# A gated feed-forward layer on one core: token halves in turn, weights read twice, x transposed on TensorE

## The chip, the core and the metric

The kernel runs on one core of a Trainium2 chip. The metric is the device time of one execution, in microseconds (us). Six runs of the kernel before have a median of 315.34 us (314.54 to 315.62). The execution that the profiler recorded took 315.47 us; from its first to its last recorded instruction (the span) it is 313.7 us.

## The reference

```
def _gelu(x):
    return jax.nn.gelu(x, approximate=True)

B, S, D, F = 32, 32, 1024, 3584        # x: (B, S, D); w_gate, w_up: (D, F); w_down: (F, D); all bf16

def reference(x, w_gate, w_up, w_down):
    return (_gelu(x @ w_gate) * (x @ w_up)) @ w_down
```

There are 1024 tokens (T). The gelu is the tanh form, which the kernel computes as G times a sigmoid of a cubic in G.

## The kernel before

Everything is laid out by hand for five engines. Each engine has its own program (`prog_sp`, `prog_pe`, `prog_act`, `prog_dve`), run in the order in which it is written; semaphores posted by `post` and awaited by `wait` tie them together. There is no planner: the order of the lines is the order of the work. All DMAs are issued from SP (SyncE), so they stand in one queue.

**Layout.** TensorE contracts over the partitions, so x is wanted transposed: `xT` holds 8 chunks of 128 features (DC = 8) by 1024 tokens. The hidden width 3584 is cut into 28 chunks of 128 (FC = 28). The weights of gate and up come in 7 groups of 4 chunks (GF = 4, NG = 7); a group is 1 MB of gate and 1 MB of up, read in pieces of 1 KB (4 x 128 columns of 2 bytes), and `wgu` holds two groups (NB = 2). `wd` holds all of w_down (7 MB, in 7 pieces), `hT` all of the hidden values.

**SP (L136 to L156).** The first instruction is one DMA that transposes all of x on the way in (L137). After it come, group by group, gate (L146), up (L147) and a piece of w_down (L134). From the third group on, SP first waits until TensorE has used the buffer (L141). At the end SP waits, for each block of 128 tokens, until both halves of its output have been copied to `osb` and writes 256 KB (L155).

**TensorE (L158 to L204).** It waits for x, then for each chunk f: it waits for the group's up weights (L165, which stand behind gate in the queue) and, from the third chunk on, until VectorE has finished chunk f-2 (L167). Then, for each of two halves of 512 tokens (`th`), 8 matmuls accumulate gate into one PSUM bank (L171) and 8 accumulate up into another (L176); each matmul loads 128x128 weights and streams 512 columns. Two chunks of two halves with two banks each fill the 8 banks. In the second stage, for each of 8 blocks of 128 tokens (`tc`) and each of 28 chunks, two matmuls (`dh` = 0, 1) of 512 columns add to two banks (L200). All in all there are 3 x 448 matmuls of 512 columns.

**ScalarE and VectorE (L206 to L265).** For one chunk and half: ScalarE squares G (L215), VectorE makes the cubic (L243), ScalarE takes the sigmoid (L223), VectorE multiplies by G (L253) and by U (L257) into `hT`. A chunk's two halves go through these steps side by side. At the end ScalarE copies the `dh` = 0 halves of the output out of PSUM (L230), VectorE the `dh` = 1 halves (L264).

## Time and profile before

| | us |
|---|---|
| median of six runs | 315.34 |
| the profiled execution, whole | 315.47 |
| its span, first to last instruction | 313.7 |
| TensorE busy with matmuls | 293.1 (93%) |
| VectorE busy | 115.7 (37%) |
| ScalarE busy | 73.0 (23%) |
| TensorE idle before its first matmul | 17.4 |
| moved by DMA | 26.42 MB |

In the profile PE is TensorE's matmuls and PEld its weight loads (which run beside matmuls), DVE is VectorE, ACT is ScalarE, POOL is GpSimd, SP is SyncE and SPq its queue of DMA issues. Matmuls are pipelined, so the mean duration of one (some 380 ns) is longer than the step from one to the next. The column of TensorE's granted clock stands at 1.00 through the whole span in this profile; at which of its levels the engine worked is therefore read from the steps between matmuls.

### The profile page before, as it was taken

The page shows a single profiled execution, that of the slowest core. Times are in us where ns is not written, and L with a number is a line of the kernel's source. Part 1 is how long each engine was busy: PE and PEld are TensorE (multiplying, and loading weights), DVE is VectorE, ACT ScalarE, POOL GpSimd, SP SyncE. Part 2 cuts the span into 40 slices and gives each one's busy share as a digit, 9 for nine tenths or more (in the row PEclk, how much of TensorE's full clock was granted, in tenths as well). Part 3 has the DMA queues.
Part 4 walks back from the last instruction along what each step waited for, and adds up shares of the span by engine and source line. Part 5 has one row for each costly group of instructions (what it writes and reads, how often), then busy time and mean ns, then how long its engine had stood idle before and what let it go on. Part 6 is the DMA issues. An engine that isn't in the chain of part 4 may idle for free.

```text
span 313.7 us, 3338 instructions
## 1 busy us (share of the span) xinstructions
PE 293.1 (93%) x1344; PEld 132.1 (42%) x1344; DVE 115.7 (37%) x176; ACT 73.0 (23%) x122; POOL 0.2 (0%) x4
## 2 busy tenths in 40 slices
PE   0079999999999999999999999999999999999995
PEld 0024444444444444444444444444444444444442
DVE  0004556666555566655556666554000000000000
ACT  1004233333223332322243333222000000000000
POOL 0000000000000000000000000000000000000000
PEclk9999999999999999999999999999999999999999
DMA  8995007401900750190065000000000000000000
GB/s 199 319 362 191 2 0 241 162 2 52 350 2 0 222 179 2 34 364 7 0 210 192 2 1 0 2 1 0 0 36 33 0 36 33 0 33 36 0 33 33
DMA packets 27647, 26.42 MB, mean 84 GB/s; under 512 B 8688, under 2 KB 23024, under 8 KB 27632
## 3 DMA queue, kind: packets, MB, share of 16 engines
q1 hardware_dynamic: 27632, 26.22, 26.0%
q8 instruction: 10, 0.16, 0.2%
q14 instruction: 5, 0.04, 0.0%
HBM read 22.02 MB, written 2.10 MB: 77 GB/s over the span
## 4 chain that ended last, share of the span: by engine, by line
PE 93%; DMA 3%; SPq 3%; DVE 0%; issue 0%
PE ps L171 31%; PE ps L176 31%; PE ps L200 31%; DMA wgu<-in_w_up_dram 3%; SPq L137 2%; DVE osb L264 0%; SPq L146 0%
## 5 line engine op out<-in xcount | busy, mean ns | idle before, releaser
L171 PE MATMUL ps<-xT,wgu 128*128 128x512 bf16 x448 | 107.5, 383 | 17.4 <-DMA wgu<-in_w_up_dram 17.4
L176 PE MATMUL ps<-xT,wgu 128*128 128x512 bf16 x448 | 107.1, 382 | 0.0
L200 PE MATMUL ps<-wd,hT 128*128 128x512 bf16 x448 | 96.9, 379 | 0.0
L243 DVE SCALAR_TENSOR_TENSOR tt<-sq,ps 128x512 f32<-128x512 f32 x56 | 38.5, 688 | 99.0 <-ACT sq L215 99.0
L171 PEld LDWEIGHTS ps<-xT,wgu 128*128 128x128 bf16 x448 | 44.1, 99 | 70.9 <-issue 19.0
L176 PEld LDWEIGHTS ps<-xT,wgu 128*128 128x128 bf16 x448 | 44.2, 99 | 54.1 <-issue 2.2
L200 PEld LDWEIGHTS ps<-wd,hT 128*128 128x128 bf16 x448 | 43.8, 98 | 52.9
L215 ACT ACTIVATE sq<-ps 128x512 f32<-128x512 f32 x56 | 33.4, 597 | 138.8 <-PE ps L171 138.8
L257 DVE TENSOR_TENSOR hT<-pp,ps 128x512 bf16<-128x512 f32 x56 | 38.5, 688 | 5.8
L253 DVE TENSOR_TENSOR pp<-sg,ps 128x512 f32<-128x512 f32 x56 | 38.1, 681 | 1.3 <-ACT sg L223 1.3
L264 DVE CAST osb<-ps 128x512 bf16<-128x512 f32 x8 | 5.5, 692 | 89.5 <-PE ps L200 89.5
L223 ACT ACTIVATE sg<-tt 128x512 f32<-128x512 f32 x56 | 35.0, 626 | 6.4 <-DVE tt L243 6.4
L230 ACT ACTIVATE osb<-ps 128x512 bf16<-128x512 f32 x8 | 4.8, 598 | 92.0 <-PE ps L200 92.0
L215 ACT ACT_TABLE_LOAD x1 | 1.3, 1283 | 0.7 <-PEq L305 0.7
L223 ACT ACT_TABLE_LOAD x1 | 1.3, 1283 | 0.0
L305 POOL MEMSET const-bfloat16-1.0<- 128x1 bf16 x1 | 0.1, 102 | 0.0
L305 POOL MEMSET const-uint8-127<- 128x1 uint8 x1 | 0.1, 102 | 0.0
L305 POOL MEMSET const-float32-1.0<- 128x1 f32 x1 | 0.1, 99 | 0.0
L305 POOL MEMSET const-float32-0.0<- 128x1 f32 x1 | 0.1, 98 | 0.2 <-issue 0.2
## 6 DMA issues: line engine op xcount, KB each, us to landing
wgu<-in_w_gate_dram SPq DMA_DIRECT2D x7, 1024.0 KB, 5.3
wgu<-in_w_up_dram SPq DMA_DIRECT2D x7, 1024.0 KB, 7.9
wd<-in_w_down_dram SPq DMA_DIRECT2D x7, 1024.0 KB, 9.9
out_dram<-osb SPq DMA_DIRECT2D x8, 256.0 KB, 2.0
xT<-in_x_dram SPq DMA_TRANSPOSE x1, 9.7
```

Source lines behind the costliest of these rows:

```text
L137: E.ins(lambda: sp.dma_start(xT[:, :, :], xf[:, :], transpose=True)).post(("x",), 16, c_x)
L171: E.ins(lambda: pe.matmul(G_bank(p, th), wslice(b, 0, dc)[:, fl:fl + 128], xT[:, dc, th * NT:(th + 1) * NT], start=(dc == 0), stop=(dc == ...
L176: E.ins(lambda: pe.matmul(U_bank(p, th), wslice(b, 1, dc)[:, fl:fl + 128], xT[:, dc, th * NT:(th + 1) * NT], start=(dc == 0), stop=(dc == ...
L200: E.ins(lambda: pe.matmul(ps[:, bank, 0:ND], hT[:, fc, tc * 128:(tc + 1) * 128], wd[:, fc, dh * ND:(dh + 1) * ND], start=(fc == 0), stop=( ...
L215: E.ins(lambda: act.activation(sq[:, r, :], G_bank(p, th), ACT.Square))
L223: E.ins(lambda: act.activation(sg[:, r, :], tt[:, r, :], ACT.Sigmoid, scale=K1))
L230: E.ins(lambda: act.activation(osb[:, tc, dh * ND:(dh + 1) * ND], ps[:, bank, 0:ND], ACT.Copy))
L243: E.ins(lambda: dve.scalar_tensor_tensor(out=tt[:, r, :], in0=sq[:, r, :], scalar=K2, in1=G_bank(p, th), op0=ALU.add, op1=ALU.mult))
L253: E.ins(lambda: dve.tensor_tensor(out=pp[:, r, :], in0=sg[:, r, :], in1=G_bank(p, th), op=ALU.mult))
L257: E.ins(lambda: dve.tensor_tensor(out=hT[:, f, sl], in0=pp[:, r, :], in1=U_bank(p, th), op=ALU.mult))
L264: E.ins(lambda: dve.tensor_copy(osb[:, tc, dh * ND:(dh + 1) * ND], ps[:, bank, 0:ND]))
L305: nc = _bacc.Bacc("TRN2", target_bir_lowering=False, num_devices=1)
```

## The change

The two halves of the tokens are no longer taken side by side within a chunk. The work of gate and up is cut into 56 units (`k`): all 28 chunks for the first 512 tokens, then all 28 for the second. A unit is 8 gate and 8 up matmuls of 512 columns, and uses two of four PSUM banks in turn. Since every weight is now needed in both passes, gate and up are read twice: 28 groups (`NQ`) of 2 chunks, each 512 KB of gate and 512 KB of up, in pieces of 512 B, in three buffers.

The first 512 tokens of x are loaded untransposed in four blocks of 128 tokens (into `osb`, which is free until the end), transposed on TensorE (32 transposes of 128x128 into four PSUM banks) and copied to `xT` by VectorE (2 copies) and ScalarE (2 copies). The second 512 tokens come by four DMA transposes, issued behind groups 6, 7, 9 and 10. Group 0 of the gate comes in two pieces, each with a semaphore. Before the transposes TensorE runs 7 (`NWARM`) matmuls on zeros; GpSimd and VectorE make the identity; ScalarE runs one small sigmoid.

The pieces of w_down are issued between the groups, each behind a wait for a unit. In the last block of tokens the two halves of the output are finished one after the other, and the second half as two matmuls of 256 columns per chunk in two banks, copied out by two engines; its two halves are written by two DMAs.

```diff
-    GF = 4 if FC % 4 == 0 else (2 if FC % 2 == 0 else 1)
-    NB = 2
+    NU = TH * FC
+    TBH = NT // 128
+    GF = 2 if FC % 2 == 0 else 1
+    NQ = TH * NG
+    NB = 3
+    WDP = 4
...
+        def kf(k):
+            return k % FC, k // FC
+        def G_bank(k):
+            return ps[:, 2 * (k % 2), 0:NT]
+        def U_bank(k):
+            return ps[:, 2 * (k % 2) + 1, 0:NT]
+        def psT(j):
+            return ps[:, 4 + j, :].bitcast(BF16)
...
+        XTQ = (6, 7, 9, 10)
...
+        def x_copy(E, kind, eng, th, j):
+            ndc = min(2, DC - 2 * j)
+            src = psT(j)[:, 0:ndc * 512].rearrange("p (a b) -> p a b", a=ndc)[:, :, 0:NT]
+            dst = xT[:, 2 * j:2 * j + ndc, th * NT:(th + 1) * NT]
+            E.wait(("T", th))
...
         def prog_sp(E, sp):
-            E.ins(lambda: sp.dma_start(xT[:, :, :], xf[:, :], transpose=True)).post(("x",), 16, c_x)
+            for pi, (t0_, n_, q_) in enumerate(XP):
...
+                    x_dma(E, sp, pi)
+            wg0_dma(E, sp)
+            wu0_dma(E, sp)
+            def group(q):
+                b = q % NB
+                if q >= NB:
+                    E.wait(("PEgrp", q - NB))
+                elif q >= 2:
+                    E.wait(("U",) + kf(q - 2))
...
+            def wd_part(j):
+                E.wait(("U",) + kf(min(NU - 1, 4 + 6 * j)))
...
+            for q in range(1, NQ):
+                if j < NWD and 4 + 6 * j < 2 * q - 5:
+                    wd_part(j)
+                    j += 1
+                group(q)
+                if q in XTQ:
+                    i = XTQ.index(q)
+                    t0 = NT + i * 128
+                    E.ins(lambda: sp.dma_start(xT[:, :, t0:t0 + 128], xf[t0:t0 + 128, :], transpose=True))
+                    E.post(("XC", 1, i), 16, c_x[TBH + i])
...
+            tc = TT - 1
+            E.wait(("E", tc, 0))
+            E.ins(lambda: sp.dma_start(of[tc * 128:(tc + 1) * 128, 0:ND], osb[:, tc, 0:ND])).post(("out", tc), 16, c_out)
+            E.wait(("E", tc, 1))
+            E.wait(("E2", tc, 1))
+            E.ins(lambda: sp.dma_start(of[tc * 128:(tc + 1) * 128, ND:D], osb[:, tc, ND:D])).post(("out2", tc), 16, c_out)
...
         def prog_pe(E, pe):
+            def transposes(th):
...
+                for tbl in range(TBH):
+                    E.wait(("x", tb))
+                    for dc in range(DC):
+                        E.ins(lambda: pe.transpose(psT(j)[:, col:col + 128],
+                                                   xnat[:, tb, dc * 128:(dc + 1) * 128], ident[:, :]))
+                E.post(("T", th))
+            def unit(k):
+                f, th = kf(k)
+                q = th * NG + f // GF
...
+                if k >= 2:
+                    E.wait(("D3",) + kf(k - 2))
...
+                    if f == 0 and th == 0 and dc % 2 == 0:
+                        E.wait(("XC", th, dc // 2))
...
+            E.wait(("zt",))
+            for i in range(NWARM):
+                E.ins(lambda: pe.matmul(ps[:, 7, :], zt[:, 0:128], zt[:, :], start=True, stop=True))
+            E.wait(("ident",))
...
+            transposes(0)
+            for k in range(NU):
+                unit(k)
...
+                order = [(fc, dh) for fc in range(FC) for dh in range(DH)]
+                if tc == TT - 1:
+                    order = [(fc, dh) for dh in range(DH) for fc in range(FC)]
...
+                    if tc == TT - 1 and dh == 1:
...
+                        E.ins(lambda: pe.matmul(ps[:, 5, 0:256], hT[:, fc, tc * 128:(tc + 1) * 128],
+                                                wd[:, fc, ND:ND + 256],
+                                                start=(fc == 0), stop=(fc == FC - 1)))
+                        E.ins(lambda: pe.matmul(ps[:, bank, 0:256], hT[:, fc, tc * 128:(tc + 1) * 128],
+                                                wd[:, fc, ND + 256:D],
+                                                start=(fc == 0), stop=(fc == FC - 1)))
...
         def prog_act(E, act):
+            E.wait(("zt",))
+            E.ins(lambda: act.activation(junk[:, 0:8], zt[:, 0:8], ACT.Sigmoid, scale=K1))
...
         def prog_dve(E, dve):
+            E.ins(lambda: dve.memset(zt[:, :], 0.0))
+            E.post(("zt",))
+            E.wait(("iota",))
+            E.ins(lambda: dve.tensor_scalar(ident[:, :], io[:, :], 128.0, None, op0=ALU.is_equal))
+            E.post(("ident",))
...
+            for k in range(NU):
+                dve_unit_a(E, dve, k)
+                dve_unit_b(E, dve, k)
```

## Rows read from the trace of the kernel before

**Rows 1.** The page: busy us, then busy tenths in 40 slices, then DMA packets.
```profile
PE 293.1 (93%) x1344; PEld 132.1 (42%) x1344; DVE 115.7 (37%) x176; ACT 73.0 (23%) x122; POOL 0.2 (0%) x4
...
PE   0079999999999999999999999999999999999995
...
DMA packets 27647, 26.42 MB, mean 84 GB/s; under 512 B 8688, under 2 KB 23024, under 8 KB 27632
```

**Rows 2.** The chain that ended last: start us, duration us, what, count.
```profile
0.73 7.55 SPq L137
...
8.97 8.25 DMA wgu<-in_w_up_dram
...
17.36 3.57 PE ps L171 x8
...
23.87 1.73 PE ps L171 x8
...
213.80 96.71 PE ps L200 x448
```

**Rows 3.** The start in order of time: start, duration, engine, line, operation, [idle before].
```profile
19.45 0.15 PEld L171 LDWEIGHTS ps<-xT,wgu 128*128 128x128 bf16 x1 [0.28 <-issue]
19.88 0.15 PEld L171 LDWEIGHTS ps<-xT,wgu 128*128 128x128 bf16 x1 [0.28 <-issue]
```

**Rows 4.** Stretches: us; PE, PEld, DVE, ACT, POOL busy; clock, DMA share, GB/s.
```profile
3.00:8.00 5.00, 0.00 (x0) 0.00 (x0) 0.00 (x0) 0.00 (x0) 0.00 (x0) 1.00 1.28 286
13.00:16.00 3.00, 0.00 (x0) 0.00 (x0) 0.00 (x0) 0.00 (x0) 0.00 (x0) 1.00 1.10 354
17.30:23.30 6.00, 5.94 (x15) 2.14 (x16) 0.69 (x1) 0.60 (x1) 0.00 (x0) 1.00 1.09 359
56.00:58.00 2.00, 2.00 (x11) 0.88 (x9) 1.90 (x3) 0.60 (x1) 0.00 (x0) 1.00 1.05 386
```

**Rows 5.** DMA issues of the page: names, count, KB each, median us to landing.
```profile
wgu<-in_w_gate_dram SPq DMA_DIRECT2D x7, 1024.0 KB, 5.3
wgu<-in_w_up_dram SPq DMA_DIRECT2D x7, 1024.0 KB, 7.9
out_dram<-osb SPq DMA_DIRECT2D x8, 256.0 KB, 2.0
```

**Rows 6.** One line's instructions: duration ns least/median/most, first and last start.
```profile
L155 SPq DMA_DIRECT2D out_dram<-osb x8: 332/332/360, 226.7 to 311.3; - x8
```

**Rows 7.** Groups by line: busy us, mean ns of one, idle before.
```profile
L171 PE MATMUL ps<-xT,wgu 128*128 128x512 bf16 x448 | 107.5, 383 | 17.4 <-DMA wgu<-in_w_up_dram 17.4
L200 PEld LDWEIGHTS ps<-wd,hT 128*128 128x128 bf16 x448 | 43.8, 98 | 52.9
L215 ACT ACTIVATE sq<-ps 128x512 f32<-128x512 f32 x56 | 33.4, 597 | 138.8 <-PE ps L171 138.8
L243 DVE SCALAR_TENSOR_TENSOR tt<-sq,ps 128x512 f32<-128x512 f32 x56 | 38.5, 688 | 99.0 <-ACT sq L215 99.0
L223 ACT ACTIVATE sg<-tt 128x512 f32<-128x512 f32 x56 | 35.0, 626 | 6.4 <-DVE tt L243 6.4
L253 DVE TENSOR_TENSOR pp<-sg,ps 128x512 f32<-128x512 f32 x56 | 38.1, 681 | 1.3 <-ACT sg L223 1.3
L257 DVE TENSOR_TENSOR hT<-pp,ps 128x512 bf16<-128x512 f32 x56 | 38.5, 688 | 5.8
```

**Rows 8.** The last chunk's second half, in order of time.
```profile
210.18 1.89 PE L171 MATMUL ps<-xT,wgu 128*128 128x512 bf16 x8
...
212.11 0.60 ACT L215 ACTIVATE sq<-ps 128x512 f32<-128x512 f32 x1 [2.86 <-PE ps L171]
```

**Rows 9.** The end in order of time.
```profile
308.82 1.67 PE L200 MATMUL ps<-wd,hT 128*128 128x512 bf16 x7
...
310.53 0.69 DVE L264 CAST osb<-ps 128x512 bf16<-128x512 f32 x1 [11.39 <-PE ps L200]
311.30 0.33 SPq L155 DMA_DIRECT2D out_dram<-osb  x1
```

## The prediction

> **What bounds the kernel now.** I read the page's busy times and slices first. TensorE is busy for 93% of the span, and its slices are full from the fourth to the last but one; the other engines are far from full [rows 1]. So there are two questions only: does TensorE ever run slower than it can, and what lies ahead of its first matmul and behind its last? The chain of waits answers both [rows 2]. SP spends 7.55 us issuing the one DMA that transposes x, then gate and up of group 0 have to land, and TensorE starts at 17.36. From 23.87 on, 8 matmuls take 1.73 us, and the 448 of the second stage take 96.71 us, which is 0.2159 us each. 1344 at this step are 290.13 us. From the first matmul to the end of the last (213.80 + 96.71 = 310.51) it is 293.15, so only 3.0 us are lost inside. The early rows say where: weight loads 0.43 us apart [rows 3] and 15 matmuls in 5.94 us [rows 4]. [...] (The column of the granted clock shows 1.00 there too, so I go by the steps.) The engine had worked for 5.9 us after standing still when it came up.

> The time is then a sum: 20.38 us ahead (17.36 + 3.02), 290.13 of matmuls, 3.19 behind the last matmul (313.7 - 310.51), and 1.77 outside the span (315.47 - 313.7). That makes 315.47, which is 0.13 above the median of 315.34.

> **The change part by part.**

> *The start.* The transposing DMA goes; in its place stand four loads of 256 KB, an issue of about 0.33 us each [rows 6]. A load of 1 MB lands 5.3 us after its issue [rows 5]; SP's first issue is at 0.73 [rows 2], so I put the fourth block at 6.0. Bounds: 2.0 us for the first 256 KB [rows 5] and three more at 386 GB/s [rows 4] give 4.8; half a microsecond of slower start gives 6.5.

> TensorE's own queue ahead of that: the zeros need one VectorE memset of 512 columns, which no row shows; between nothing and the 0.69 of VectorE's other 512-column work [rows 7], I take 0.5 and start the 7 warming matmuls at 1.3. At 0.427 each they end at 4.3. GpSimd's iota and the identity are hidden if both are done by then; iota is not in the trace, and with 0.69 for the identity it may take 2.9 us before it costs anything. By 4.3 two blocks of x lie ready. A transpose streams 128 columns: 0.107 us at the slow step, 0.054 at the fast one (a quarter of 0.427 and 0.216). All at the long step and without gaps, 32 of them end at 4.3 + 3.4 = 7.7; fast, the last eight end 0.4 behind the landing, at 6.4. I take 7.3, nearer the slow end, because the clock in before came up only 5.9 us after the first matmul, and 1.3 + 5.9 = 7.2.

> Copies of 1024 columns out of PSUM: between 0.60 and 1.38 us (a 512-column ScalarE operation, and twice a VectorE one [rows 7]); I take 1.2, and 0.1 for two hand-offs. Unit 0 starts at 8.6. Its fifth matmul needs the second pair of copies, 1.2 us later, while four fast matmuls last 0.86: a stall of 0.4 (0 if the clock is slow). Gate of group 0 has landed by about 7.5 and up by 9.0 to 9.7 (2 MB land 0.4 + 7.9 us after the first issue [rows 5], up to 0.7 more in smaller pieces), before 10.7, when it is first needed. For the clock I add 0.3. Ahead: 8.6 + 0.4 + 0.3 = 9.3 instead of 20.38.

> *The middle.* The number of 512-column matmuls stays 1344; gate and up are read twice. Group 1 and the later ones, w_down and the second half of x make 29.4 + 7.3 + 1.0 = 37.7 MB in 56 units of 3.454 us (16 steps), 193.4 us: 195 GB/s. Pieces of 512 B are not in the trace. The pieces on either side are: 1 KB (gate, up) at 354 GB/s, and x at 286 [rows 4], whose 8192 small packets (those below 512 B, of 8688 [rows 1]) carry 2.1 MB, 256 B each. So between 286 and 354, I take 300, and it is hidden. TensorE itself doesn't slow while DMA moves 386 GB/s: 11 matmuls begin or run in 2 us, all of it busy [rows 4]. [...] The four transposing DMAs take SP some 0.9 us each (an eighth of 7.55); behind each waits the next group, which is not due for another 6.9 us. SP has the same slack with the moved pieces of w_down: each waits for a unit that is already past when the wait is reached.

> *The new wait per unit.* Unit k waits for VectorE to finish unit k-2 (before it was a chunk of two halves, twice that distance). The chain after G's last matmul is 0.597 + 0.688 + 0.626 + 0.681 + 0.688 = 3.28 [rows 7] and four hand-offs of 0.04 (the matmuls end at 212.07, the square starts at 212.11 [rows 8]): 3.44. G ends 1.89 us into its unit, so the chain ends at 5.33 and unit k+2 begins at 6.91: 1.6 us to spare, cost nothing. Behind that wait stands all of TensorE's work; every microsecond of the chain beyond 1.6 would be paid up to 54 times.

> *The end.* The last block's second half runs as 56 matmuls of 256 columns. [...] After the last matmul: the copy of 512 columns (0.69 [rows 9]) becomes 256, between 0.35 and 0.69, I take 0.45; a write of 256 KB lands in 2.0 [rows 5], 128 KB saves up to 0.37, I take 1.7. Behind: 3.19 - 0.24 - 0.3 = 2.65.

> **Sum:** 9.3 + 290.13 + 0.07 + 2.65 + 1.77 = 303.9 us.

> **The rivals.**

> B, *the clock is still down when unit 0 begins.* Nothing in the trace says whether transposes, and the wait for copies after them, do what 5.9 us of dense matmuls did; the warming matmuls alone are 3.0 us. Then the transposes end at 7.7, unit 0 begins at 9.0, and 14 matmuls at the long step are paid again (2.95; the 0.4 of stall goes): 12.0 ahead, 306.6 us. For it: those 5.9 us. Against: TensorE would be without a long gap from 1.3 to 7.7. Its own range is 305.2 to 307.8.

> C, *transposes don't overlap.* A matmul lasts 383 ns while the step is 216 [rows 7]; if each transpose pays the 167 between them and 107 of columns, 32 cost 8.8 us, end at 13.1, and unit 0 begins at 14.4; with 0.4 of stall and half of the 3.0 for the clock, 310.9 us. A late identity looks the same. Against it: the loads and matmuls of all 1344 are pipelined. [...]

> D, *the weights come too late.* If the second reading and the 512 B pieces held DMA below 195 GB/s, every group after the first few would be waited for. At 184 GB/s (37.7 MB in 193.4 + 11.5 us) the gain is gone; at 150 the stage takes 251 us and the whole 362 us. Against it: 286 GB/s with pieces half as long.

> E, *the wait per unit bites a little*: 0.1 us over in each of 54 units is 5.4, 309.3 us; it needs a chain of 5.1 us where rows give 3.4.

> **How the numbers follow.** Forecast 0.48, B 0.32, C 0.11, E 0.05, D 0.03, and 0.01 for no change by several of these at once. Predicted: 303.9. The forecast's own range: early landing and fast copies (unit 0 at 7.3, no clock loss) give 302.2; the late ends of both (unit 0 at 9.4, 0.5 more for the clock) 305.2. The whole range reaches over B and its bounds, and leaves out most of C, E and D: 302.0 to 308.5. A measurement of this kernel can't tell less than about 0.2% (0.6 us) from no change. Forecast, B, C and E are faster: 0.96; within 0.2%: 0.01; D, slower: 0.03.

> **What would show it.** [...] Wrong: matmuls 0.43 us apart in units 0 and 1 (B); transposes more than 0.15 us apart (C); TensorE released by a weights DMA again and again, with the DMA slices full (D); short idle times before each unit that VectorE ends (E).

## The result, and the profile after

The changed kernel takes 303.35 us (median of 8 executions, 303.00 to 303.78), the one before 315.16 (16 executions): a ratio of 0.9628, with an interval of 0.9618 to 0.9638. 303.9 had been forecast. The profiled execution took 303.29 us, its span is 301.5. Of all the executions timed for this document one, with the old end described below, took 1802.93 us, and its run's ratio leaves it out.

The page of the changed kernel: busy us, then the slices, then DMA. They answer to [rows 1].

```profile
PE 296.6 (98%) x1411; PEld 137.8 (46%) x1411; DVE 122.5 (41%) x180; ACT 77.2 (26%) x125; POOL 0.4 (0%) x5
...
PE   8899999999999999999999999999999999999996
...
DMA packets 68065, 41.13 MB, mean 136 GB/s; under 512 B 5456, under 2 KB 63056, under 8 KB 68048
```

TensorE is full from the third slice on, with 14.7 MB more moved beside it. The chain of the changed kernel (start, duration, what) answers to [rows 2]:

```profile
2.11 0.43 SPq L183
...
3.61 6.67 DMA wgu<-in_w_up_dram
...
10.32 1.90 PE ps L293 x8
12.22 1.73 PE ps L287 x8
...
202.16 90.65 PE ps L343 x420
292.81 0.11 PE ps L336
```

From 12.22 on, 8 matmuls take 1.73 us, to the end of the first stage. Only the first up matmuls of unit 0 wait for a DMA. The chain goes from SP's issues through the landing of up to these matmuls; x, its transposes and its copies are not on it. The start of the changed kernel, in order of time, shows the pieces of its lead:

```profile
0.82 0.24 POOL L248 IOTA io<- 128x128 f32 x1 [0.38 <-POOLq L481]
0.86 0.27 DVE L414 MEMSET zt<- 128x256 uint32 x1 [0.86 <-PEq L481]
1.19 3.17 PE L301 MATMUL ps<-zt 128*128 128x512 bf16 x7 [1.19 <-DVE zt L414]
4.46 2.97 PE L263 MATMUL ps<-ident,osb 128*128 128x128 bf16 x32
7.47 1.29 DVE L194 COPY xT<-ps 128x1024 bf16<-128x1024 bf16 x2 [6.14 <-PE ps L263]
7.47 1.94 ACT L192 ACTIVATE xT<-ps 128x1024 bf16<-128x1024 bf16 x2 [5.23 <-PE ps L263]
8.22 1.90 PE L287 MATMUL ps<-xT,wgu 128*128 128x512 bf16 x8 [0.79 <-DVE xT L194]
10.32 1.90 PE L293 MATMUL ps<-xT,wgu 128*128 128x512 bf16 x8 [0.21 <-DMA wgu<-in_w_up_dram]
```

Unit 0 begins at 8.22 instead of 17.36, and at the short step: 8 matmuls take 1.90 us, of which the last lasts 0.38, so they begin 0.217 apart. Its 8 gate matmuls have run their steps at 9.95 (8.22 + 8 x 0.2159); its up matmuls begin at 10.32, a wait of 0.37 us (the 0.21 of the row counts from the last matmul's end). 8 steps before 10.32 is 8.59, the lead that answers to 20.38 before. Two stretches of the transposes show where the steps became shorter (us; PE and PEld busy with counts):

```profile
4.46:6.60 2.14, 2.14 (x21) 2.14 (x22) 0.00 (x0) 0.00 (x0) 0.00 (x0) 1.00 1.02 325
6.60:7.40 0.80, 0.80 (x14) 0.66 (x11) 0.00 (x0) 0.00 (x0) 0.00 (x0) 1.00 1.12 329
```

Some 20 transposes take 0.107 us each, a quarter of the 0.427 of the long step (in the kernel before, weight loads at 17.74 and at 22.86 lie 12 steps apart); the others come closer together. TensorE had worked since 1.19, with a pause of 0.1. The column of the granted clock stands at 1.00 in both stretches. That the long step is that of a lower clock is therefore my reading of the steps; in the run with all of x first the column shows a lower value beside such steps, 0.50. The steps don't become short at the same time in every execution: in a second profiled one of the same kernel (e11_after_beside, below) the transposes come 0.056 us apart from the first one on, and then wait for the last block of x:

```profile
4.35 1.50 PE L263 MATMUL ps<-ident,osb 128*128 128x128 bf16 x24
...
6.19 0.62 PE L263 MATMUL ps<-ident,osb 128*128 128x128 bf16 x8 [0.34 <-DMA osb<-in_x_dram]
...
7.59 1.90 PE L287 MATMUL ps<-xT,wgu 128*128 128x512 bf16 x8 [0.79 <-DVE xT L194]
...
9.82 1.90 PE L293 MATMUL ps<-xT,wgu 128*128 128x512 bf16 x8 [0.32 <-DMA wgu<-in_w_up_dram]
```

Unit 0 begins 0.6 us earlier there, and TensorE still waits for up, which lands at 9.77 instead of 10.28. The two executions took 302.78 and 303.29 us: the 0.51 between them is what lies between the two landings. So in both it is the landing of up that ends the start.

The end in order of time answers to [rows 9]:

```profile
298.95 0.38 ACT L410 ACTIVATE osb<-ps 128x256 bf16<-128x256 f32 x1 [5.51 <-PE ps L339]
298.96 0.42 DVE L435 CAST osb<-ps 128x256 bf16<-128x256 f32 x1 [11.46 <-PE ps L339]
299.41 0.33 SPq L244 DMA_DIRECT2D out_dram<-osb  x1
```

The last matmul ends at 298.93, so 2.57 us lie behind it (3.19 before). The sum after: 8.59 ahead, 290.13 of matmuls at full step, 0.07 for the short ones, 2.57 behind, 1.79 outside the span: 303.15. The 0.14 that is missing from 303.29 is the middle, where 1308 matmuls take 282.49 instead of 282.4, and rounding. Of the 12.2 us between the two profiled executions the start gave 11.8.

Compared with [rows 2], these 11.8 us are four pieces, with 0.1 left over: up of group 0 is issued 5.4 us earlier (3.61, was 8.97) and lands 1.6 us sooner after its issue (6.67, was 8.25); the first 8 gate matmuls no longer wait for it (1.7); and no matmul of a unit runs at the long step (3.0). Why up lands sooner is not shown: no run takes apart the groups of half the size and the plain loads of x ahead of them.

### The profile page after: what moved, and what is told of

Its sections match the earlier page's. It is cut to its first block, busy times and chain, and to the rows that moved or that the text cites. A ratio compares the mean times of both kernels' runs of the same rounds, so it can differ in the third digit from the quotient of the medians.

```text
span 301.5 us, 3567 instructions
## 1 busy us (share of the span) xinstructions
PE 296.6 (98%) x1411; PEld 137.8 (46%) x1411; DVE 122.5 (41%) x180; ACT 77.2 (26%) x125; POOL 0.4 (0%) x5
## 4 chain that ended last, share of the span: by engine, by line
PE 96%; DMA 2%; SPq 1%; DVE 0%; issue 0%
PE ps L293 32%; PE ps L287 31%; PE ps L343 30%; DMA wgu<-in_w_up_dram 2%; PE ps L339 1%; PE ps L336 1%; SPq L183 1%; SPq L174 0%; DVE osb L435 0%
## 5 line engine op out<-in xcount | busy, mean ns | idle before, releaser
L287 PE MATMUL ps<-xT,wgu 128*128 128x512 bf16 x448 | 105.8, 379 | 0.8 <-DVE xT L194 0.8
L293 PE MATMUL ps<-xT,wgu 128*128 128x512 bf16 x448 | 105.8, 379 | 0.2 <-DMA wgu<-in_w_up_dram 0.2
L343 PE MATMUL ps<-wd,hT 128*128 128x512 bf16 x420 | 90.8, 379 | 0.0
L343 PEld LDWEIGHTS ps<-wd,hT 128*128 128x128 bf16 x420 | 41.1, 98 | 49.6
L435 DVE CAST osb<-ps 128x512 bf16<-128x512 f32 (+1 forms) x8 | 5.3, 658 | 90.2 <-PE ps L343 78.7
L339 PE MATMUL ps<-wd,hT 128*128 128x256 bf16 x28 | 6.2, 273 | 0.0
L336 PE MATMUL ps<-wd,hT 128*128 128x256 bf16 x28 | 6.2, 272 | 0.0
L301 PE MATMUL ps<-zt 128*128 128x512 bf16 x7 | 3.2, 630 | 1.2 <-DVE zt L414 1.2
L194 DVE COPY xT<-ps 128x1024 bf16<-128x1024 bf16 x2 | 1.3, 687 | 6.1 <-PE ps L263 6.1
L192 ACT ACTIVATE xT<-ps 128x1024 bf16<-128x1024 bf16 x2 | 1.9, 1021 | 5.2 <-PE ps L263 5.2
L263 PEld LDWEIGHTS ps<-ident,osb 128*128 128x128 bf16 x32 | 2.8, 128 | 1.0 <-issue 1.0
L263 PE MATMUL ps<-ident,osb 128*128 128x128 bf16 x32 | 3.0, 277 | 0.1
L336 PEld LDWEIGHTS ps<-wd,hT 128*128 128x128 bf16 x28 | 2.7, 98 | 0.4
L339 PEld LDWEIGHTS ps<-wd,hT 128*128 128x128 bf16 x28 | 2.7, 98 | 0.4
```

The lines of the kernel that those rows point to most:

```text
L263: E.ins(lambda: pe.transpose(psT(j)[:, col:col + 128], xnat[:, tb, dc * 128:(dc + 1) * 128], ident[:, :]))
L287: E.ins(lambda: pe.matmul(G_bank(k), wslice(b, 0, dc)[:, fl:fl + 128], xT[:, dc, tsl], start=(dc == 0), stop=(dc == DC - 1)))
L293: E.ins(lambda: pe.matmul(U_bank(k), wslice(b, 1, dc)[:, fl:fl + 128], xT[:, dc, tsl], start=(dc == 0), stop=(dc == DC - 1)))
L336: E.ins(lambda: pe.matmul(ps[:, 5, 0:256], hT[:, fc, tc * 128:(tc + 1) * 128], wd[:, fc, ND:ND + 256], start=(fc == 0), stop=(fc == FC - 1)))
L339: E.ins(lambda: pe.matmul(ps[:, bank, 0:256], hT[:, fc, tc * 128:(tc + 1) * 128], wd[:, fc, ND + 256:D], start=(fc == 0), stop=(fc == FC - ...
L343: E.ins(lambda: pe.matmul(ps[:, bank, 0:ND], hT[:, fc, tc * 128:(tc + 1) * 128], wd[:, fc, dh * ND:(dh + 1) * ND], start=(fc == 0), stop=( ...
```

## The experiments

**The clock alone.** The kernel before, with nothing added but 56 warming matmuls (NWARM).

```diff
         def prog_pe(E, pe):
+            E.wait(("zt",))
+            for i in range(NWARM):
+                E.ins(lambda: pe.matmul(ps[:, 7, :], zt[:, 0:128], zt[:, :], start=True, stop=True))
...
```

> The kernel before, with one thing of the change alone: 56 matmuls of 512 columns on zeros run on TensorE from about 1.2 us on, while x and the first weights are on their way. Nothing else moves. My theory: of the 11.8 us that the start gained, 2.9 to 3.0 us are the clock alone (14 matmuls at 0.427 instead of 0.216 us), the rest is that x and the first weights arrive earlier. So unit 0 still begins at 17.4 us, but steps of 0.216 from its first matmul on, and the time is 312.2 to 312.5 us. Rival: the gap of about 1 us between the warming matmuls and the real ones lets the clock fall, or the first matmuls were held up by the DMA beside them and not by the clock; then it stays at 315.2.

Measured: 312.78 us against 315.08 (ratio 0.9935, 0.9914 to 0.9955), a little more than the 312.2 to 312.5 of the theory. The chain of this run:

```profile
9.26 8.56 DMA wgu<-in_w_up_dram
...
17.96 1.89 PE ps L178 x8
19.84 1.73 PE ps L183 x8
```

The steps are 0.216 from the first real matmul, although TensorE had paused for 1.8 us ahead of it. In this execution the weights landed 0.6 us later than in [rows 2]; that is where the rest of the 2.95 went in its profile. So 2.3 (1.4 to 2.7) of the gain can be had without any new order, and the rival is refuted for this execution. One of the six took 314.38 us, at a mean granted clock of 0.995 where the others have 0.999 or 1.000; it has no trace, so where in it the clock was lower is not shown.

**No warming matmuls**, run twice.

```diff
-    NWARM=7,
+    NWARM=0,
```

> The changed kernel without its 7 warming matmuls (NWARM = 0); the transposes and all the rest stay. Theory 1 (transposes do for the clock what matmuls of 512 columns do): transposes begin when the first block of x lands, at 3.4 us, end with the last block at about 7.6, and the clock comes up some 5.5 us after their first, at about 9: unit 0 begins at 8.4 and pays 2 to 4 matmuls at the long step, partly under the wait for copies and for up: 303.6 to 304.2 us. Theory 2 (rival B of the prediction: transposes do nothing for the clock): unit 0 begins at 8.4 at the long step, 13 to 14 matmuls are paid, 2.7 to 2.95 us: 305.8 to 306.2 us.

> The changed kernel without its warming matmuls once more: of six executions two took 305.4 us and four 302.7 to 303.1. My theory: whether transposes, with the gaps between them, bring the clock up before unit 0 differs from execution to execution; so the times again fall into two groups 2.3 to 2.7 us apart, and the profiled one shows 0.107 us steps to the end of the transposes and 0.427 in unit 0 if it is of the upper group, and 0.216 from unit 0 on if it is of the lower. Rival: the upper two were something else of that chip; then all times lie within 0.8 us.

Measured: 303.10 us (305.44, 305.38 and four from 302.67 to 303.14), and in the second job 305.58 (304.59 to 305.84). So there are two groups, and neither theory of the first run holds for all executions; the second run, with all four in the upper group, didn't show both groups within one job, as its theory had it. Both profiled executions are of the upper group; the chain of the first:

```profile
1.64 4.47 DMA osb<-in_x_dram
...
6.16 1.90 PE ps L263 x16
...
8.83 3.59 PE ps L287 x8
12.42 1.94 PE ps L293 x8
```

TensorE waits for the third block of x, 16 transposes take 1.90 us, the long step, and then 8 matmuls take 3.59 us and the next 8 still 0.2 more than 1.73: some 9 at the long step of 0.427, by an estimate from these times (5.53 us in all instead of 1.90 + 1.73, and 0.211 for each). This is the mechanism of rival B at a lower price than its 2.7 us over 14 matmuls. Against the changed kernel's profile unit 0 begins 0.6 later, 9 matmuls at the long step cost 1.9, and the wait for up (0.4) goes; the two profiled executions are 2.15 and 2.04 us longer. (The two groups of the first job are 2.5 apart.) That the steps were short in time in the lower group is inferred from the times; no trace of such an execution was taken. The 7 warming matmuls don't make the kernel faster than its best without them; they keep it out of the upper group: none of the 12 timed executions with them, in two jobs, took more than 303.8. The chip doesn't explain it either: in the very jobs of these two runs the kernel with the old end (303.43 to 303.81, but for the one execution named above) and the one with half a MB more traffic (303.20 to 303.70), both with the 7 matmuls, show no upper group.

**The old end** under the new start: both halves of the last block side by side, one write of 256 KB.

```diff
-                if tc == TT - 1:
-                    order = [(fc, dh) for dh in range(DH) for fc in range(FC)]
...
-                    if tc == TT - 1 and dh == 1:
+                    if False:
...
```

> The changed kernel with the end of the kernel before: the last block's two halves side by side, 512 columns each, one copy per engine and one write of 256 KB. My theory: the new end is worth 0.5 to 0.65 us (copy 0.69 instead of 0.42, landing 2.0 instead of 1.7, less 0.07 for the shorter matmuls): 303.8 to 304.0 us. Rival: the write's latency is what counts and does not depend on its size, and the copy's gain is eaten by 56 shorter matmuls: 303.2 to 303.5.

Measured: 303.71 us, a ratio of 0.9637 (0.9620 to 0.9654) to the kernel before in its job; the median lies between the two forecasts and the interval overlaps the changed kernel's, so the times alone don't decide. The trace does for its own execution:

```profile
298.12 0.59 PE L335 MATMUL ps<-wd,hT 128*128 128x512 bf16 x2
298.54 0.60 ACT L397 ACTIVATE osb<-ps 128x512 bf16<-128x512 f32 x1 [11.49 <-PE ps L335]
298.75 0.69 DVE L422 CAST osb<-ps 128x512 bf16<-128x512 f32 x1 [11.39 <-PE ps L335]
```

The last matmul ends at 298.71 and the span at 301.9: 3.19 us, exactly as before the change, against 2.57. Less the 0.07 of short matmuls, the end is worth 0.55.

**The first half of x by DMA transposes** instead of TensorE's.

```diff
-    NWARM=7,
+    NWARM=26,
...
-            E.ins(lambda: eng.dma_start(xnat[:, t0_:t0_ + n_, :], src))
+            E.ins(lambda: eng.dma_start(xT[:, :, t0_ * 128:(t0_ + 1) * 128], xf[t0_ * 128:(t0_ + 1) * 128, :], transpose=True))
...
-            transposes(0)
+            for i in range(TBH):
+                E.wait(("x", i))
...
```

> The changed kernel, but its first 512 tokens come by four DMA transposes ahead of the first weights, as the second 512 do later; no transposes on TensorE and no copies, 26 warming matmuls bridge the time. My theory: what keeps the first weights back is SP's time for issuing transposing DMAs (7.55 us for 1024 tokens in the kernel before; 2.2 to 3.1 us for each 128 tokens in the changed kernel, in mid-stream): between 3.8 and 10.5 us before the first weights are issued, so up lands at 11 to 18 instead of 10.3, and the time is 304.5 to 311 us. Rival: only that half of x is wanted first did the work, and the transposes on TensorE are no better than those of the DMA: 302.5 to 303.5 us.

Measured: 306.26 us (ratio 0.9724, 0.9705 to 0.9744), 2.9 more than the changed kernel. Its chain:

```profile
0.74 1.35 SPq L183
...
4.82 1.31 SPq L183
...
6.17 0.58 SPq L174
...
7.35 5.50 DMA wgu<-in_w_up_dram
...
12.90 1.90 PE ps L291 x8
```

SP needs 1.3 us per block for issuing a transposing DMA, 0.4 for a plain one; so up is issued at 7.35 instead of 3.61. It lands 1.2 us sooner after its issue than in the changed kernel, at 12.85 instead of 10.28, and these 2.6 us are the whole difference between the two profiled executions (305.87 and 303.29). What costs is SP's issue time. The rival is refuted; and 9 of the 12 us are there without TensorE's transposes, with 26 warming matmuls ahead of unit 0, whose matmuls run at the short step (8 for up in 1.90 us).

**All of x first**, eight blocks and 64 transposes.

```diff
-        XP = [(tb, 1, "sp") for tb in range(TBH)]
+        XP = [(tb, 1, "sp") for tb in range(TT)]
...
-        XTQ = (6, 7, 9, 10)
+        XTQ = ()
...
             transposes(0)
+            transposes(1)
...
```

> The changed kernel, but all of x comes first: eight blocks of 128 tokens instead of four ahead of the first weights, 64 transposes on TensorE and 8 copies instead of 32 and 4, and no DMA transposes later. Everything else stays. It asks what wanting only half of x first is worth. My theory: the landing sets the start; 1 MB more at some 350 GB/s is 2.8 to 3.0 us more until gate and up of group 0 land, so unit 0 begins at 11 to 11.5 instead of 8.2 and the time is 306.0 to 306.6 us. Rival: TensorE's and the copies' own work sets it; 32 more transposes at 0.054 us and four copies beside them are 1.7 to 2.3 us: 305.0 to 305.7 us. If neither half matters, 303.4.

Measured: 307.25 us (305.70 to 308.02), more than either theory gave. The chain:

```profile
4.46 2.60 PE ps L263 x32
...
7.09 1.95 ACT xT L192 x2
...
9.28 3.45 PE ps L263 x32
12.73 1.73 PE ps L287 x8
```

Gate and up are not waited for at all, so the landing, my theory, doesn't set this start. The second 32 transposes need the PSUM banks that the copies empty, 2.2 us of standstill, and then run at the long step, 32 in 3.45 us. Here the column of the granted clock shows it too (the last three numbers are the clock, the DMA share and GB/s):

```profile
9.28:10.50 1.22, 1.22 (x12) 1.22 (x13) 0.00 (x0) 0.00 (x0) 0.00 (x0) 0.50 1.19 303
```

The mean over the span is 0.994, which is what 0.50 for these 3.45 us and 1.00 for the rest of the 305.5 would give; from 12.73 on 8 matmuls take 1.73 us again. 32 transposes at the long step instead of the other are 1.7 us; without that the profiled execution would have come to an estimated 305.6, in the rival's range. Of the two executions with a mean clock of 1.000 one is in it (305.70) and one is not (306.80); the three at 0.994 took 307.25 to 308.02. The run shows that asking for all of x first costs some 4 us in this form; it doesn't show what a form with more banks would cost.

**More DMA traffic**, half a MB (NX = 1) and one (NX = 2) behind each group.

```diff
+                for i in range(NX):
+                    if q > 2:
+                        E.wait(("xt", q - 1, i))
+                    if q >= 2:
+                        E.ins(lambda: sp.dma_start(xtra[:, i * DC:(i + 1) * DC, :], src_g)).post(("xt", q, i), 16, c_xt[i])
...
```

> The changed kernel with more DMA traffic and nothing else: behind each of groups 2 to 27, 512 KB of gate are read once more into a buffer that nobody uses (26 x 0.52 = 13.6 MB). The stage of 193 us then asks for 51.3 MB, 265 GB/s, instead of 195. My theory: the weights have room (the stretches in which DMA was busy moved 286 to 354 GB/s), so 303.2 to 303.7 us. Rival (D of the prediction, nearer than I thought): DMA was close to its bound with pieces of 512 B; at 230 GB/s the stage would take 223 us and the whole 333 us.

> The same with 1 MB more behind each of groups 2 to 27: 65 MB in the stage, 336 GB/s. My theory: this is past what pieces of 512 B can bring, some 290 to 320 GB/s, so TensorE waits for gate or up in group after group, the stage takes 203 to 224 us and the whole 313 to 334 us, which shows that rival D is a real mechanism with its edge between the two runs. If DMA can move 340 GB/s in such pieces, it stays at 303.5.

Measured: 303.54 us (303.20 to 303.70) with half a MB, 333.39 (ratio 1.0616) with one. The stage in one stretch, first with half, then with one MB:

```profile
12.00:203.00 191.00, 191.00 (x887) 86.61 (x885) 113.68 (x166) 67.44 (x110) 0.00 (x0) 1.00 1.01 260
```

```profile
20.00:213.00 193.00, 172.50 (x768) 74.75 (x767) 99.00 (x144) 58.57 (x97) 0.00 (x0) 0.97 1.18 296
```

At 260 GB/s TensorE is busy in all of 191 us. In the second run the demand is some 330 GB/s (the 265 and 336 of the expectations count group 0 as well) and DMA delivers 296. TensorE stands still for 20 us of the 193, and the granted clock falls to 0.97 on average; the 768 matmuls would take 165.8 us at the full step, so 27 us are lost in all. Rival D is a real mechanism, with its edge between 260 and 296 GB/s for this mix of pieces; the change, which moves 189 in this stage, stands at least 70 below it. SP's own wait for the extra reads is too short to be the cause:

```profile
SPq L222 <- DMA xtra<-in_w_gate_dram: 4.4, 19, 0.4
```

(us in total, times, longest). With half a MB TensorE waits for gate and for up once each in the whole run, 0.9 and 0.7 us.

**A shorter start**, in two forms. The line of `XP` is in the first form alone.

```diff
-    NWARM=7,
+    NWARM=5,
...
-        XP = [(tb, 1, "sp") for tb in range(TBH)]
+        XP = [(tb, 1, "sp" if tb % 2 == 0 else "act") for tb in range(TBH)]
...
-            E.wait(("T", th))
+            E.wait(("T", th, j))
...
+                        if tbl == TBH - 1 and dc % 2 == 1:
+                            E.post(("T", th, j))
...
-            for k in range(NU):
+            unit(0, u=False)
+            unit(1, u=False)
+            unit(0, g=False)
+            unit(1, g=False)
+            for k in range(2, NU):
                 unit(k)
...
+            for j in (0, 2, 3):
+                x_copy(E, "dve", dve, 0, j)
...
```

> The changed kernel with its start shortened where the trace shows it waiting: two of the four x blocks are issued from ScalarE's queue, so that SP comes to the weights 0.9 us earlier; 5 warming matmuls instead of 7, so that the first transposes begin when the first block lands (3.3) and not at 4.46; each PSUM bank is copied as soon as its own last transpose is done; VectorE copies three of the four banks (0.65 each against 1.0 on ScalarE); and the gate matmuls of units 0 and 1 run before their up matmuls, so that up, which lands last, is wanted 1.7 us later. My theory: the transposes end at 6.6 to 6.9 instead of 7.4, unit 0 begins at 7.2 to 7.5 instead of 8.2, and nothing waits behind it: 1.0 to 1.3 us off, 302.0 to 302.4 us. Rival: the landing of x and gate is what sets the start, two queues share the same 16 engines and bring nothing earlier; only the 0.2 us of wait for up and 0.3 of copies go: 302.7 to 303.0 us.

> The shortened start of the run e7 with one thing undone: all four x blocks are issued from SP again, one after the other. In e7 the first block landed 3.3 us after its issue instead of 2.6, since two blocks shared the DMA engines, and TensorE stood still for 0.7 us ahead of the transposes. My theory: now the first block is there when the five warming matmuls end at 3.5, the transposes end at 6.9 to 7.3, and unit 0 begins at 7.5 to 7.9 with gate landing as in the changed kernel (8.6 for its second piece, wanted 0.9 after the start of the unit): 302.6 to 303.0 us. Rival: the last block and the second piece of gate land as late as ever, so that unit 0 gains nothing over the changed kernel but the copies' 0.3: 303.0 to 303.3.

Measured: 303.09 us with two queues for x (ratio 0.9637, 0.9619 to 0.9655), no measurable gain. The rival gave about the right size (302.7 to 303.0) for a wrong reason: the last block did land earlier, at 5.6 (issued at 1.2, 4.4 us to landing) instead of 6.7. But the first came later, 3.32 us after its issue, as its chain shows, and the transposes, from 4.19 on, ran at the long step to their end, 0.107 us apart from 4.19 to 7.5 (the chain follows 26 of the 32):

```profile
0.74 3.32 DMA osb<-in_x_dram
...
4.19 2.95 PE ps L263 x26
...
7.91 3.74 PE ps L288 x16
```

With x from SP alone 302.49 (0.9613, 0.9597 to 0.9629), just below its theory's 302.6 to 303.0. The first block landed 2.8 us after its issue there; that the two blocks of the other form shared the DMA engines was my explanation, and the runs show only the times. To compare directly, the latter and the changed kernel were run side by side:

> The changed kernel itself, unaltered, on the same chip and in the same rounds as the shortened start of e10, to compare the two directly. Expected: 303.0 to 303.7 us, as before.

> The shortened start of e10 once more, beside the changed kernel. My theory: it is 0.6 to 0.9 us faster (8.2 of lead instead of 8.6, and fewer executions in which the clock or the landing come late): 302.3 to 302.8 us. Rival: the difference between the two jobs was the chip; then the two agree within 0.3 us.

Measured: 302.96 (302.78 to 303.06) for the changed kernel and 302.23 (301.88 to 303.65) for the shorter start, 0.7 apart in the medians; but one of its five executions was slower than all of the other's, and the intervals of the two ratios (0.9605 to 0.9646, 0.9587 to 0.9641) overlap. The chain of the shorter start:

```profile
2.12 4.29 DMA osb<-in_x_dram
...
6.77 0.70 DVE xT L194
...
7.52 3.64 PE ps L288 x16
11.16 3.02 PE ps L297 x14
```

Here the last x block ends the wait; gate and up of units 0 and 1 then run through, with 0.2 us of stall. It is probably the best of all, by 0.2%, but that is near what these measurements can tell.

## Why the prediction was right

The forecast was the likeliest case, and it came: 303.9 against 303.35. That the lead is what the change shortens was right, and so were the terms of the matmuls, the middle and the end. The lead itself came near (8.59 against 9.3) on another path than the one it was added up on, and that is partly luck.

- *What bounds the kernel.* It was the lead: 11.8 of 12.2 us. The long steps' part of it, 2.95 by 14 matmuls at 0.427 instead of 0.216, was measured alone as 2.3 (1.4 to 2.7).
- *The path of the start.* The sum followed x: its landing, the transposes, the copies. It took up as landed by 9.0 to 9.7, before it is needed at 10.7. In the two profiled executions up landed at 10.28 and 9.77 and was wanted at 9.95 and 9.32, so SP's seven issues and the landing of up set the lead.
- *The landing of x*: the fourth block landed at 6.7 (2.11 and 4.6 from issue to landing, the longest of four), not 6.0, and even past the late bound of 6.5; in e11 at 6.1. In the first execution that cost nothing: the 32 transposes ran without a break. An issue took 0.42 us, not the 0.33 of a write.
- *The transposes* ended at 7.43 (7.3 forecast). The warming matmuls began at 1.19 (1.3), and the steps were short before unit 0 (the last of the two stretches above has 14 transposes in 0.80 us). The 0.3 added for the clock was not needed.
- *The copies* were the term that was mis-sized: VectorE's took 0.69 us for 1024 columns of bf16 from PSUM, as long as 512 columns of fp32 take in [rows 9], and not the 1.2 I took; ScalarE's took 1.02. Unit 0 so began at 8.22 instead of 8.6. The stall of 0.4 that was forecast for the second pair of copies did not occur: the 8 gate matmuls take 1.90 us, as the 8 up matmuls behind them do. The 0.37 that stands in its place is all wait for up, the same size by luck.
- *The middle* cost nothing. For the unit whose gate begins at 98.39 VectorE's last step ended at 103.81, and the unit that waits for it began at 105.30: 1.49 us to spare, 1.6 forecast. Rival E had no room, and behind unit 0 no wait of TensorE for VectorE stands in the trace. The 29.4 MB of the weights counted all 28 groups; without group 0 they are 28.3, so the demand was 190 GB/s, and 189 were moved.
- *The transposing DMAs* took SP 2.2 to 3.1 us in mid-stream, not 0.9. It did no harm, because the group behind each was not due: behind unit 0's wait for up, no wait of TensorE for gate or up stands in the trace.
- *The end*: 2.57 (2.65). The 0.07 that the sum has for the short matmuls was my estimate, and no run of the kernel before shows it. In the changed kernel their 28 pairs begin 0.2185 us apart (292.64 to 298.54, 27 steps), 0.0026 more than the 0.2159 of one matmul of 512 columns: 0.07 in all.
- *Rivals.* B's mechanism exists, but needs the warming matmuls taken away, and cost 2.0 to 2.2 us instead of 2.7 in the executions that were profiled. C fell: one transpose lasts 277 ns, yet 32 end in 2.97 us. The 277 is a mean of some 311 ns at the long step and some 219 at the other; it is no step. D was measured: 300 GB/s had been taken for 512 B pieces, 296 came, with 2 KB pieces of w_down among them.

The groups of the changed kernel's page behind the copies and the transposes (busy us, mean ns of one), and the least, median and longest duration of a transpose in ns:

```profile
L194 DVE COPY xT<-ps 128x1024 bf16<-128x1024 bf16 x2 | 1.3, 687 | 6.1 <-PE ps L263 6.1
L192 ACT ACTIVATE xT<-ps 128x1024 bf16<-128x1024 bf16 x2 | 1.9, 1021 | 5.2 <-PE ps L263 5.2
...
L263 PE MATMUL ps<-ident,osb 128*128 128x128 bf16 x32 | 3.0, 277 | 0.1
```

```profile
L263 PE MATMUL ps<-ident,osb x32: 219/311/311, 4.5 to 7.2; 128*128 128x128 bf16 x32
```

## What to carry to other kernels

When one engine is full from its first instruction to its last, look only at its lead and its tail, and write the lead as a list of landings: which bytes does the first instruction need, in which order does the queue bring them, and how long does each issue hold the queue. Then ask which landing ends last: here it was not x, on which the work was done, but the weights queued behind it. Reading weights twice, so that half of the activations suffice at the start, cost nothing here: the stage moved 189 GB/s, and nothing was lost up to 260. For another kernel, measure that edge by adding traffic. Warming matmuls were worth having for steadiness, though the best execution didn't need them: with them none of 12 executions took more than 303.8 us, without them six of ten took 304.59 or more.
